# Ordering the crossed products of a half-chunk visit: a drain of TensorE in place of one-column ScalarE copies

## The chip, the cores and the metric

The kernel runs on one core of a Trainium2 chip. The metric is the device time of one execution in microseconds (us): the median of several executions, lower is better. The engines have the names that the profile gives them: PE is TensorE (matrix products), PEld its weight loads, ACT ScalarE, DVE VectorE, POOL GpSimd, SP the engine that issues most of the transfers. A q behind a name (PEldq, ACTq) means the engine's sequencer: instructions that never reach the engine's data path.

## The reference, cut to what matters

A retention layer over 4 batches, 8 heads, 768 positions and 64 channels a head is followed by two feed-forward layers (an ELU of width 2048, then a maximum over three products of width 768). Only the first concerns the change:

```python
for t in range(S):
    state = gamma * state + outer(k[:, :, t], v[:, :, t])
    y[:, :, t] = scale * (q[:, :, t] @ state)
```

## The kernel before

**Chunks and visits.** The recurrence is worked off in 24 chunks of 128 positions (6 chunks for each of 4 batches, taken batch by batch in turn, so that chunk c belongs to batch c % 4). Chunks 0 to 3 have no past and go through wider code at the start. Chunks 4 to 23 are worked in two halves of 64 positions with products of 64x64 tiles, four of which fit into the array of TensorE side by side. Such a half-chunk visit has these steps:

- `scores` (products at L207) and `update` (L235) of the chunk: keys times queries, and keys times values, both into the same two PSUM banks (tile `xs`).
- `mask` (DVE, L221), `decay` (POOL, L250), `advance` (DVE, L256 and L258) and `queries_of` (POOL, L194): the masked scores, the two states, and the decayed queries.
- `value_products` (L276 and, through `past(c, 0)`, L265): values times masked scores, then the straight part of queries times states, into two more PSUM banks, also named `xs`, one for each half s.
- `watch` (ACT, L289): one column of each of these two banks is copied into a spare column of `cols_sb`. Nothing reads the copies. They read the banks, so the crossed products that come next have to wait for them, and they themselves wait for the straight products.
- `finish_products` (L265 again, through `past(c, 1)`): the crossed part of queries times states is added into the same banks. The half s of the output now takes its rows from the other group of 64 rows of the array: `s = g ^ cross`. So a tile of another row group adds to the same PSUM columns as in the straight part.
- `finish_copies` and `finish_low` (L309, L316, L333) or `finish_row` (L1776): the result leaves PSUM.

One execution has 20 such visits. Each records 16 crossed products (16 instructions on PE at L265 and as many weight loads).

**The order of the work.** Chunks 4 to 7 stand in an order written out by hand (the string `FIRST`: V is `value_products`, gd is `watch`, F is `finish_products`, S and U are `scores` and `update`). Chunks 8 to 23 are put in order by a planner that has a cost and a due time for each step. It runs when the program is built; on the chip each engine has one fixed queue. In the plan a visit is

```python
def visit(c):
    value_steps(c)
    ...
        open_steps(c + 1)
    finish_steps(c)
```

with these steps for the copies and the crossed products:

```python
add("A", 0.42, lambda: watch(c), xs, [("seen", c)])
...
add("P", 0.45, lambda: finish_products(c), [("seen", c), mid, qd], xs + [("free", 0), ("home", c % CB)])
```

So between the straight and the crossed products of chunk c the queue of PE mostly has `scores` and `update` of chunk c + 1, which is small tiles again. In some visits the step just ahead of the crossed products is instead a product of a feed-forward layer, of the full 128x128 array with 512 columns (L481, L491, L504, L555). These full products fill the rest of PE's queue. L447 is ScalarE's half of the conversion of a weight, which full products at L491 wait for.

Of the kernel before, what the change touches and what calls it, by code (L numbers as in the profile page):

```python
# [78 lines left out]
def kernel(ctx: ExitStack, tc: tile.TileContext, qkv0, qkv, wa, wb, dmask, qdec, cols, out):  # L79


    nc = tc.nc
# [19 lines left out]
    guard = cols_sb[:, H + 2 * NPAIR:]  # L102
# [45 lines left out]
    def rows(i):  # L148
        return slice(i * HC, (i + 1) * HC)

    def heads():
        return [(2 * i + g, g, r, 2 * i + r) for i in range(2) for r in range(2) for g in range(2)]
# [107 lines left out]
    def past(c, cross):  # L260
        qd = st_t[c]
        for p, g, r, n in heads():
            s = g ^ cross
            src = middle if s else home[c % CB]
            nc.tensor.matmul(  # L265
                xo_t[c][s][rows(r), p, :], src[rows(g), n, :], qd[rows(g), n, s * HC:(s + 1) * HC],
                start=False, stop=p // 2 == 1, skip_group_check=True,
            )
# [13 lines left out]
    def values(c):  # L282
        value_products(c, twin()[0])
        watch(c)

    def watch(c):
        xs = xo_t[c]
        for s in range(2):
            nc.scalar.copy(guard[:, s:s + 1], xs[s][:, 0, 0:1])  # L289

    def finish(c):
        finish_high(c)
# [2 lines left out]
    def finish_high(c):  # L295
        finish_products(c)
        finish_copies(c)

    def finish_products(c):
        past(c, 1)  # L300
        if c // CB < NCH - 1:
            home[c % CB], free_state[0] = free_state[0], home[c % CB]
        del raw_t[c], st_t[c]
# [1256 lines left out]
    def low_copies():  # L1560
# [7 lines left out]
        "Uw": wide_update, "hm": wide_home, "S": early_scores, "K": keys_of, "U": lambda c: update(c, twins.pop(c)),  # L1568
        "M": mask, "mid": decay, "C": advance, "Q": queries_of, "V": lambda c: value_products(c, twin()[0]),
        "gd": watch, "F": finish_products, "xh": finish_copies, "xl": finish_low, "qk": lambda c: load(c, "qk"),  # L1570
        "k": lambda c: load(c, "k"), "v": lambda c: load(c, "v"), "kv": lambda c: load(c, "kv"),
        "bi": cv_bits, "sh": cv_shift, "sg": cv_sign, "tl": cv_tail, "hi": cv_high, "lo": cv_low,
# [171 lines left out]
    def value_steps(c):  # L1744
        su, a, mid, qd = opened[c]
        banks = [bank() for _ in range(2)]
        xs = [x for x, _ in banks]
        add(
            "P", 0.82, lambda: value_products(c, twin()[0]), [kv_of(c), a, mid, qd, ("home", c % CB)], xs,
            [x for _, x in banks],  # L1750
        )
        add("A", 0.42, lambda: watch(c), xs, [("seen", c)])
        opened[c] = xs, mid, qd

    def finish_steps(c):
        xs, mid, qd = opened[c]
        add("P", 0.45, lambda: finish_products(c), [("seen", c), mid, qd], xs + [("free", 0), ("home", c % CB)])
        late_c = c >= DEFER
        if c // CB == 3:
            for s in range(2):  # L1760
                add("A", 0.8, lambda s=s: finish_row(c, s), xs[s:s + 1], [("row", c, s)], [("X", 0)])
            if c % CB == CB - 1:
                for x in ("a21", "a22"):
                    plan.add("Q", 0.0, None, [("row", k, s) for k in range(c - CB + 1, c + 1) for s in range(2)], [("source", "a", x)])
        elif late_c:
            x, x0, _ = e_ring()
            add("A", 0.9, lambda: finish_high(c), xs, [x], [x0])
            add("S", 0.42, lambda: store_late(c), [x], [("xd", c)], move=(32, 0.032))
        else:
            add("A", 0.66, lambda: finish_high(c), xs, [("xh", c)], [("X", c // CB - 2)])  # L1770
            add("D", 0.76, lambda: finish_low(c), xs + [("xh", c)], [("xl", c)], [("X", c // CB - 2)])
# [333 lines left out]
```

## Time and profile before

| what | us |
| --- | --- |
| median of 3 executions (lowest, highest) | 946.17 (945.87, 948.68) |
| the profiled execution, its own time | 947.08 |
| span of its trace, first to last instruction | 945.3 |

The visits of chunks 4 to 7 lie between 30 and 57 us of the span, those of chunks 8 to 23 between 133 and 400 us; after that there are no half-chunk visits. In the rows below, times are in us from the start of the span. Engines work side by side, so that a busy engine matters for the time where the others wait for it in the end. A row of the timeline that merges several instructions gives the start of the first and the length to the end of the last.

### The profile page before, as it was taken

To read this page: it belongs to the slowest core of one execution; us is meant where nothing else is said; L and a number is where in the kernel's file an instruction comes from. 1 tells how busy PE (TensorE), PEld (TensorE's weight loads), DVE (VectorE), ACT (ScalarE), POOL (GpSimd) and SP (SyncE) were. 2 spreads that over 40 slices of the span, in tenths; PEclk is the share of its full clock that TensorE was granted. 3 is DMA by queue.
4 is the path that set the end of the run, shared out by engine and by line. 5 is a ranking of instruction groups with operands and counts; after the bars stand their busy time and mean duration, and the time that the engine had idled before them with its cause. 6 is when DMAs were issued, how large, how long until landed. Compare 5 with 4: busy or idle time off the path is not lost.

```text
span 945.3 us, 16772 instructions
## 1 busy us (share of the span) xinstructions
PE 932.2 (99%) x6553; PEld 764.1 (81%) x6553; DVE 653.5 (69%) x1009; ACT 379.8 (40%) x694; POOL 246.3 (26%) x346
## 2 busy tenths in 40 slices
PE   7999999999999999999999999999999999999998
PEld 5778888778788888888888888888888888888886
DVE  6897777667687576688668885898725777246651
ACT  3566554545564454556446663222311113101110
POOL 2510022554445245312333341345000100001000
PEclk9999999999999999999999999999999999999999
DMA  9924366789779498679777797989636564345602
GB/s 312 337 94 166 118 210 205 257 241 290 204 210 282 160 269 256 175 235 304 219 200 221 204 280 252 282 227 247 236 114 242 185 205 134 112 156 183 206 1 89
DMA packets 108351, 196.67 MB, mean 208 GB/s; under 512 B 8560, under 2 KB 53616, under 8 KB 104048
## 3 DMA queue, kind: packets, MB, share of 16 engines
q1 hardware_dynamic: 77296, 112.22, 36.3%
q0 software_dynamic: 29680, 80.76, 30.3%
q10 hardware_dynamic: 1296, 2.62, 0.8%
q8 instruction: 52, 0.85, 0.4%
q14 instruction: 27, 0.22, 0.1%
HBM read 141.30 MB, written 54.26 MB: 207 GB/s over the span
## 4 chain that ended last, share of the span: by engine, by line
PE 92%; DMA 3%; DVE 1%; issue 1%; POOL 1%; SPq 1%; ACT 1%; POOLq 0%; DVEq 0%
PE acc L555 22%; PE hp L1412 18%; PE hp L1204 12%; PE acc L1472 10%; PE acc L491 6%; PE hp L481 5%; PE hp L504 4%; PE acc L1313 3%; PE hp L1313 3%; PE hp L1268 2%; PE xs L276 1%; PE xs L265 1%; DMA ops_a<-t 1%; PE acc L1204 1%; PE xs L207 1%
## 5 line engine op out<-in xcount | busy, mean ns | idle before, releaser
L1412 PE MATMUL hp<-seat,w 128*128 128x512 f32 x798 | 182.4, 389 | 0.1
L1412 PEld LDWEIGHTS hp<-seat,w 128*128 128x128 f32 x798 | 149.6, 188 | 31.7 <-DMA w<-ops_d 0.5
L555 PE MATMUL acc<-gh,w 128*128 128x512 f32 x600 | 150.5, 392 | 0.0
L555 PEld LDWEIGHTS acc<-gh,w 128*128 128x128 f32 x600 | 111.7, 188 | 23.8 <-ACT gh L537 0.3
L1021 POOL DMA_DIRECT2D w<-ops_d x95 | 50.8, 537 | 280.1 <-PE hp L1412 209.9
L1204 PE MATMUL hp<-seat,w 128*128 128x512 f32 x504 | 115.9, 389 | 0.0
L1204 PEld LDWEIGHTS hp<-seat,w 128*128 128x128 f32 x504 | 94.6, 188 | 19.6
L1472 PE MATMUL acc<-w,g 128*128 128x512 f32 x432 | 99.1, 389 | 0.0
L1472 PEld LDWEIGHTS acc<-w,g 128*128 128x128 f32 x432 | 81.1, 188 | 16.8
L555 PE MATMUL acc<-gl,w 128*128 128x512 f32 x300 | 81.2, 390 | 0.0
L1010 POOL DMA_DIRECT2D w<-ops_a x91 | 49.4, 544 | 87.4 <-PE hp L1204 64.9
L555 PEld LDWEIGHTS acc<-gl,w 128*128 128x128 f32 x300 | 56.2, 188 | 11.8
L1438 ACT COPY u<-hp 128x512 f32<-128x512 f32 x19 | 11.2, 587 | 103.1 <-PE hp L1412 103.1
L184 POOL TENSOR_TENSOR x<-x,cols_sb 128x512 f32<-128x512 f32 x24 | 28.6, 1194 | 91.4 <-DMA x<-in_qkv 91.3
L541 DVE TENSOR_TENSOR gl<-e,gh 128x512 fp32r<-128x512 f32 x59 | 44.5, 755 | 9.9 <-ACT gh L537 4.1
L537 ACT CAST gh<-e 128x512 fp32r<-128x512 f32 x59 | 36.5, 619 | 33.7 <-PE acc L555 13.7
L874 POOL TENSOR_TENSOR t<-t 128x256 f32<-128x256 f32 x36 | 32.6, 906 | 66.3 <-DVE m L918 48.6
L491 PE MATMUL acc<-gh,w 128*128 128x512 f32 x168 | 44.8, 396 | 0.4 <-ACT gh L537 0.4
L504 PE MATMUL hp<-xh,w 128*128 128x512 f32 x120 | 39.4, 391 | 0.0
L1313 PE MATMUL hp<-seat,w 128*128 128x512 f32 x168 | 38.9, 390 | 0.0
L1313 PE MATMUL acc<-seat,w 128*128 128x512 f32 x168 | 38.7, 389 | 0.0
L541 DVE TENSOR_TENSOR gl<-hold,gh 128x512 fp32r<-128x512 f32 x32 | 24.5, 766 | 20.5 <-PE acc L555 20.3
(182 smaller groups left out, 1600.6 us busy)
## 6 DMA issues: line engine op xcount, KB each, us to landing
w<-ops_d POOLq DMA_DIRECT2D x33, 1024.0 KB, 5.2
w<-ops_a POOLq DMA_DIRECT2D x91, 256.0 KB, 4.3
x<-in_qkv SPq DMA_DIRECT2D x44, 512.0 KB, 5.8
ops_d<-m SPq DMA_DIRECT2D x66, 256.0 KB, 4.2
raw<-in_wa SPq DMA_DIRECT2D x32, 512.0 KB, 6.1
w<-ops_d POOLq DMA_DIRECT2D x63, 256.0 KB, 4.6
raw<-in_wb SPq DMA_DIRECT2D x24, 512.0 KB, 5.2
ops_a<-w SPq DMA_DIRECT2D x24, 256.0 KB, 3.7
```

Of the source, the lines that this page charges most:

```text
L481: nc.tensor.matmul(hp_t[b, f], w_t[0, f // 2][:, f % 2, pw, kk * P:(kk + 1) * P], x_t[b][px][:, kk, :], start=i == 0 and kk == 0, stop=i = ...
L491: nc.tensor.matmul(acc_t[b, f0][m], w_t[1, f // 2][:, f % 2, pw, m * P:(m + 1) * P], g_t[b, f][pg], start=f == f0 and i == 0, stop=f == f1 ...
L504: nc.tensor.matmul(hp, w[:, pw, kk * P:(kk + 1) * P], x[px][:, kk, :], start=k == 0, stop=k == len(order) - 1,)
L537: nc.scalar.copy(gh, e_t[b, f])
L541: nc.vector.tensor_tensor(out=gl, in0=e_t.pop((b, f)), in1=f32(gh), op=ALU.subtract)
L555: nc.tensor.matmul(acc_t[b, f0][m], w[:, p[0], m * P:(m + 1) * P], g[p[1]], start=f == f0 and p == first, stop=f == f1 - 1 and p == final, ...
L1010: nc.gpsimd.dma_start(out=live_slot(j).rearrange("p h t -> p (h t)"), in_=ops_a[:, j % AHEAD].rearrange("p h t -> p (h t)"))
L1021: nc.gpsimd.dma_start(out=group_tile(n)[:, a:z].rearrange("p s h t -> p (s h t)"), in_=ops_d[:, 4 * k + a:4 * k + z].rearrange("p s h t -> ...
L1204: nc.tensor.matmul(ps[name], w[:, pw, kk * P:(kk + 1) * P], x[px][:, kk, :], start=first and k == 0, stop=last and k == 5, skip_group_chec ...
L1313: nc.tensor.matmul(ps[name], w[:, pw, kk * P:(kk + 1) * P], x[px][:, kk, :], start=first and i == 0, stop=last and i == 5, skip_group_chec ...
L1412: nc.tensor.matmul(o, w[:, pw, kk * P:(kk + 1) * P], x[px][:, kk, :], start=first and k == 0, stop=last and k == 5, skip_group_check=True,)
L1472: nc.tensor.matmul(acc, g2[f][:, px, m * P:(m + 1) * P], w[:, pw, :], start=f == 0 and i == 0, stop=f == KF2 - 1 and i == 2, skip_group_ch ...
```

## The change

The step `watch` keeps its place and its cost in the plan but issues nothing. `finish_products` begins with a drain on TensorE's queue.

```diff
     def watch(c):
         xs = xo_t[c]
-        for s in range(2):
-            nc.scalar.copy(guard[:, s:s + 1], xs[s][:, 0, 0:1])
+        pass
...
     def finish_products(c):
+        nc.tensor.drain()
         past(c, 1)
         if c // CB < NCH - 1:
             home[c % CB], free_state[0] = free_state[0], home[c % CB]
```

## Rows read from the trace of the kernel before

**Rows 1.** The page: busy time and share of each engine, PE clock, chain

```profile
PE 932.2 (99%) x6553; PEld 764.1 (81%) x6553; DVE 653.5 (69%) x1009; ACT 379.8 (40%) x694; POOL 246.3 (26%) x346
...
PEclk9999999999999999999999999999999999999999
...
PE 92%; DMA 3%; DVE 1%; issue 1%; POOL 1%; SPq 1%; ACT 1%; POOLq 0%; DVEq 0%
```

**Rows 2.** Busy time by stretch: stretch, length, then PE busy (instructions) first

```profile
60.00:237.00 177.00, 176.23 (x1708) 143.84 (x1707) 132.38 (x216) 97.01 (x194) 50.70 (x52) 1.00 0.67 208
237.00:260.00 23.00, 21.79 (x222) 17.59 (x224) 15.20 (x26) 12.82 (x26) 10.43 (x16) 1.00 0.71 199
260.00:400.00 140.00, 139.96 (x1436) 115.60 (x1437) 98.86 (x151) 69.39 (x138) 57.37 (x78) 1.00 0.77 225
```

**Rows 3.** The copies' line: engine, operation, count, shortest/median/longest ns

```profile
L289 ACT COPY cols_sb<-xs x40: 141/160/167, 31.7 to 397.3; 128x1 f32<-128x1 f32 x40
```

**Rows 4.** PE's waits, 60 us to the end: total us, times, longest

```profile
PE xs L276 <- DVE e L1166: 0.9, 1, 0.9
PE xs L265 <- ACT cols_sb L289: 0.9, 2, 0.6
PE xs L207 <- DVE e L529: 0.2, 1, 0.2
```

**Rows 5.** Timeline around the crossed products of chunk 18: start, length, instruction

```profile
298.60 0.22 ACT L289 COPY cols_sb<-xs 128x1 f32<-128x1 f32 x2 [0.24 <-PE xs L265]
...
299.22 0.14 PEld L265 LDWEIGHTS xs<-qd,dmask_sb 64*64 64x64 f32 x1
...
299.29 0.22 PE L235 MATMUL xs<-x 64*64 64x64 f32 x1
299.34 0.40 PE L265 MATMUL xs<-qd,dmask_sb 64*64 64x64 f32 x14
299.67 0.50 PE L555 MATMUL acc<-gh,w 128*128 128x512 f32 x1
```

**Rows 6.** Timeline, the drains and the last products at the program's end

```profile
940.62 0.84 PE L1472 MATMUL acc<-w,g 128*128 128x512 f32 x3
941.50 0.37 ACT L1485 COPY o<-acc 128x256 f32<-128x256 f32 x1 [3.45 <-PE acc L1472]
```

**Rows 7.** PE's drains in the prologue and at the end: ns, first and last start

```profile
L2096 PEldq DRAIN x1: 8/8/8, 0.3 to 0.3; - x1
...
L2101 PEldq DRAIN x2: 13/2140/4267, 937.2 to 944.8; - x2
```

**Rows 8.** The chain of waits around the crossed products of chunk 16

```profile
258.81 0.28 PE xs L265 x13
259.10 0.21 ACT cols_sb L289 x2
259.31 0.04 issue
259.35 0.46 PE xs L265 x16
```

**Rows 9.** The same pattern as rows 5, its first and last place: chunks 8 and 22

```profile
135.55 0.22 PE L265 MATMUL xs<-qd,dmask_sb 64*64 64x64 f32 x1
135.56 0.22 PE L235 MATMUL xs<-x 64*64 64x64 f32 x1
...
390.13 0.22 PE L265 MATMUL xs<-qd,dmask_sb 64*64 64x64 f32 x1
390.13 0.22 PE L235 MATMUL xs<-x 64*64 64x64 f32 x2
```

**Rows 10.** Timeline before the crossed products of chunk 23

```profile
398.14 1.08 PE L555 MATMUL acc<-gh,w 128*128 128x512 f32 x4
399.15 0.29 PE L265 MATMUL xs<-qd,dmask_sb 64*64 64x64 f32 x4
...
399.15 0.15 PEld L265 LDWEIGHTS xs<-qd,dmask_sb 64*64 64x64 f32 x4 [0.36 <-issue]
```

**Rows 11.** The chain around the crossed products of chunk 5

```profile
42.80 0.46 PE xs L265 x16
43.26 0.02 issue
43.28 0.38 ACT xh L316
43.66 0.02 issue
43.69 0.76 DVE xl L333 x2
```

**Rows 12.** Timeline around the crossed products of chunk 6

```profile
47.86 0.64 PE L207 MATMUL xs<-x 64*64 64x64 f32 x30
...
49.04 0.50 PE L491 MATMUL acc<-gl,w 128*128 128x512 f32 x1 [0.24 <-DVE gl L541]
```

**Rows 13.** The chain around the crossed products of chunk 13

```profile
189.26 0.11 ACT cols_sb L289 x2
189.37 0.53 ACT w L447
189.90 0.04 issue
189.94 3.04 PE acc L491 x12
```

## Prediction

> **What bounds the kernel now.** I read the page first. PE is busy 932.2 us of a span of 945.3 us, its clock is at the top level in every slice, and the chain that ended last runs over PE for 92% of the span [rows 1]. The busy times by stretch then show how little room PE leaves where the planned visits lie: it is idle 0.8 us in the 177 us up to 237 us, 1.2 us in the next 23 us, and 0.04 us in the 140 us from 260 to 400 us [rows 2]. So in these stretches a step that holds PE for 0.1 us costs the kernel 0.1 us, and a step taken from another engine gains only what PE had waited for it. That is the key to the whole case: ScalarE is at 40% [rows 1], and what it is relieved of has no value of its own.
>
> Next I read what the copies cost. There are 40 of about 160 ns, two in each of the 20 visits [rows 3]. Together that is 40 x 0.16 = 6.4 us of ScalarE. PE waited for them twice after 60 us, 0.9 us in all; its only other two waits there came from VectorE, 0.9 and 0.2 us [rows 4]. In the other visits the copies were done long before PE came to the crossed products. In chunk 18 they run from 298.60 to 298.82, and the crossed products' first weights are loaded at 299.22 [rows 5]: scores and update of the next chunk lie between and cover the copies.
>
> **The change, part by part.**
>
> **The price of a drain.** The trace has drains on PE, at the program's two ends. With nothing in flight one took 8 ns, another 13 ns [rows 7]. The one at 937.2 us took 4.27 us and so ended at about 941.5 us [rows 7]; the last product of the program ends at 940.62 + 0.84 = 941.46 [rows 6]. So the drain was taken up by the sequencer four microseconds ahead of the array, and it ended when the last result was in, not when the last product had been issued. How long after, the rows give to 0.05 us only; ScalarE, which waits for the same product, starts 0.04 us after its end [rows 6], and I take 0.04 us for the drain too. Behind it the sequencer has to start again. The nearest row is PE's start behind the copies in chunk 16: the copies end at 259.31, the crossed products start 0.04 us later [rows 8]. I take 0.04 us for that as well. The drain's tail and restart then are 0.08 us, on top of the wait until the products in flight have ended. From below the bound is 0: results in, next load at once. From above I take the longest idle time that the rows show in front of a first weight load that waits for no other engine, 0.36 us [rows 10], with 0.04 us ahead of it, 0.40 us.
>
> **Eleven visits where small tiles run ahead** (chunks 8 to 11, 14 and 17 to 22; rows 5 show one, rows 9 the first and the last). The crossed products now overlap the update's: their weights are loaded at 299.22, while the last update product runs from 299.29 to 299.51, and all of the crossed ones end at 299.74 [rows 5]. Behind a drain they start at 299.51 + 0.08 = 299.59. Started from a standstill the 16 take 0.46 us [rows 8], so they end at 300.05 in place of 299.74: 0.31 us. Nothing covers this, since the full product at 299.67 [rows 5] stands behind them in PE's queue. Eleven times 0.31 is **+3.4 us** (0.23 x 11 = 2.5 with the lower bound, 0.63 x 11 = 6.9 with the upper).
>
> **Six visits where a full product runs ahead** (chunks 4, 5, 7, 12, 15 and 23). In chunk 23 the last full product ends at 399.22 and the crossed products' weights are loaded from 399.15 on [rows 10]. The array is changed from one tile size to the other here, and the overlap is only 0.07 us. With the drain the load comes at 399.22 + 0.08 = 399.30: 0.15 us, six times **+0.9 us** (0.4 to 2.8). The Trainium skill, "TensorEngine Tiling (Array Packing)", section Key Properties, says that a change of the tiling mode drains TensorE by itself; by it these six drains would add nothing. The overlap of 0.07 us in the modelled ends neither proves nor excludes that; it is a rival below. For the early ones delay is not hidden either: behind chunk 5 the chain itself leads from the crossed products over ScalarE's and VectorE's copies back to PE [rows 11].
>
> **Chunk 6: nothing.** Its predecessor, a run of score products, ends at 48.50; with 0.08 and 0.46 us behind it the crossed ones end at 49.04, which is when PE went on anyway, after a wait of 0.24 us for VectorE [rows 12]. With the upper bound it would cost 0.3 us.
>
> **The two visits where PE waited for the copies.** In chunk 16 the straight products end at 259.09 and the crossed ones started at 259.35 [rows 8]; behind a drain they start at 259.17, so I count **-0.2 us**. In chunk 13 PE waits for ScalarE in any case: the full products behind the crossed ones need a converted weight, which ends the chain at 189.90, and the copies stand ahead of it on ScalarE with 0.11 us of the chain [rows 13]. That is all there is to gain: **-0.1 us**. The wait of 0.5 us ahead of these crossed products was covered by that one, and so is the drain.
>
> **What is queued behind a drain.** PE's own products and weight loads, and the sequencer's waits; nobody waits for the drain itself. The copies out of the banks, the next decay on POOL and the load of the chunk after next wait for the crossed products and move with them. They keep their distance to PE's later steps, which move by the same amount. The 6.4 us taken from ScalarE hide beside PE and I cost them at nothing apart from the 0.1 us above; if PE were not the bound they would matter.
>
> **The sum** is 3.4 + 0.9 - 0.2 - 0.1 = +4.0 us. Against the profiled execution's own 947.08 us, of which 945.3 us are the span, this gives 951.1 us. That execution is 0.9 us above the median of the three runs, 946.17 us; against the median it gives **950.2 us**, 0.42% more. A difference under 0.3%, 2.8 us, can't be told from none.
>
> **The rivals.**
>
> *The tile size's own drain.* If a change of tile size empties the array already, six drains are free, and the sum is 3.1 us: 949.3 us. For it speaks that the load ahead of the crossed products stands idle for 0.36 us there [rows 10], against it the overlap of 0.07 us.
>
> *The drain does not hold the array.* If in mid-stream it ends when the products ahead of it are issued, it costs the sequencer 8 to 13 ns [rows 7], which its head start covers, and only gains are left: 0.1 us of chunk 13 and, in chunk 16, the whole time from 258.81 + 0.28 = 259.09 to 259.35 and the overlap of about 0.25 us that rows 5 show for unhindered crossed products. That is -0.6 us, 945.6 us, not slower than before. It is decided at the eleven small-tile places: by whether the crossed products still start 0.01 us ahead of the last update product [rows 9]. Against it speaks the drain of 4.27 us [rows 7].
>
> *The restart is dear.* The drain takes the sequencer's head start away; if each first load behind it comes as late as in rows 10, the upper bound holds: 6.9 + 2.8 + 0.3 us, little gained in chunk 16 either, together about +9.9 us, 956.1 us. Against it: PE's restart of 0.04 us behind the copies [rows 8], though there the products were already queued behind the wait.
>
> *ScalarE's relief reaches PE.* If other waits of PE shrank because ScalarE is free sooner and the drains were nearly free, the 2.0 us of rows 4 would be all that can go: 944.2 us. Three of them end on other engines' work or are counted above.
>
> **How the numbers follow.** The forecast has 0.57, the tile size's own drain 0.15, the drain that does not hold 0.10, the dear restart 0.13, ScalarE's relief 0.05. By 2.8 us slower are the dear restart (0.13), nine tenths of the forecast (0.51) and half of the tile-size case (0.08): 0.72. Faster by more than that would need more than all of PE's waits after 60 us; runs that scatter and the relief leave 0.04. The rest, 0.24, is within 0.3%. The range reaches from 946.5 us, which leaves out most of the drain that does not hold and the relief, to 953.5 us, which takes in a restart of up to 0.25 us a drain and leaves out the dear one at its full price. The forecast alone would lie between 948.7 us (lower bounds: 2.5 + 0.4 - 0.3 - 0.1 = +2.5) and 951.5 us.
>
> **What would show it.** Right: 20 drains on PE's sequencer that end just behind the last product ahead of them; at the eleven small-tile places the first crossed load 0.05 to 0.1 us after the last update product's end, and 0.3 us more from the straight products to the next full one; no overlap of crossed and other small products anywhere; no copies at L289, and no PE wait for them; nothing new between 400 us and the end. Wrong: an unbroken stream across the drain; a gap of 0.3 us or more between a drain's end and the first load; a new wait of PE for another engine behind the crossed products; or gaps at full-product places as long as at the small ones.

## The result and the profile after

The changed kernel takes 952.76 us, the median of 4 runs (952.44 to 953.82), beside 946.44 us of the kernel before on the same chip (4 runs, 945.87 to 948.68). The medians differ by 6.3 us. The ratio as recorded is 1.0061, with a 95% interval of 1.0045 to 1.0077: worked out from it, the change is 5.8 us (4.3 to 7.3) slower. The profiled execution of the changed kernel took 953.82 us, with a span of 952.1 us; that is 6.8 us longer than the span of the kernel before, 945.3 us.

The page of the changed kernel, engines and chain (it answers to [rows 1]):

```profile
PE 936.3 (98%) x6553; PEld 766.5 (81%) x6553; DVE 654.4 (69%) x1009; ACT 375.8 (39%) x654; POOL 247.3 (26%) x346
...
PE 94%; DMA 2%; SPq 1%; DVE 1%; issue 1%; ACT 1%; POOL 0%; POOLq 0%; DVEq 0%; ACTq 0%
```

ScalarE has 40 instructions and 4.0 us less and PE has the same 6553 products, but 4.1 us more busy time, and drains are not counted as busy; where that comes from is seen below. First the drain's line in the changed kernel (duration shortest/median/longest in ns, first and last start), for the whole program and then for chunk 18 alone:

```profile
L299 PEldq DRAIN  x20: 475/525/3752, 31.6 to 403.8; - x20
...
L299 PEldq DRAIN  x1: 517/517/517, 304.2 to 304.2; - x1
```

The sequencer waits 0.5 us in a typical drain. That is not its price: most of it is time in which the array still works off what was issued. The price is read from the array's own stream. Timeline of the changed kernel around the crossed products of chunk 18 (PE), with their first weight load (PEld); it answers to [rows 5]:

```profile
304.21 0.46 PE L235 MATMUL xs<-x 64*64 64x64 f32 x18
304.81 0.46 PE L265 MATMUL xs<-qd,dmask_sb 64*64 64x64 f32 x16
305.20 0.50 PE L555 MATMUL acc<-gh,w 128*128 128x512 f32 x1
...
304.80 0.15 PEld L265 LDWEIGHTS xs<-qd,dmask_sb 64*64 64x64 f32 x4 [0.28 <-issue]
```

The update's last product ends at 304.21 + 0.46 = 304.67. The crossed products' weights used to be loaded 0.29 us ahead of that end [rows 5]; now they are loaded 0.13 us behind it. From that end to the full product behind was 0.16 us before (299.51 to 299.67); it is 305.20 - 304.67 = 0.53 us now. This place cost 0.37 us.

The same view of the changed kernel at chunk 23, where a full product runs ahead (answers to [rows 10]):

```profile
405.53 0.62 PE L555 MATMUL acc<-gh,w 128*128 128x512 f32 x2
406.24 0.29 PE L265 MATMUL xs<-qd,dmask_sb 64*64 64x64 f32 x4
...
406.23 0.15 PEld L265 LDWEIGHTS xs<-qd,dmask_sb 64*64 64x64 f32 x3 [0.51 <-issue]
```

The full product ends at 406.15 and the load comes 0.08 us behind it; before, it came 0.07 us ahead: 0.15 us.

PE's waits in the changed kernel from 60 us on (total us, times, longest; answers to [rows 4]):

```profile
PE xs L276 <- DVE e L1166: 1.9, 1, 1.9
PE acc L491 <- ACT w L447: 0.5, 1, 0.5
PE xs L265 <- issue: 0.5, 3, 0.2
PE xs L207 <- DVE e L529: 0.2, 1, 0.2
```

The wait for the copies is gone. Its 0.6 us of chunk 13 came back in the line for ScalarE's converted weight (L447), which stood right behind it. The wait for VectorE ahead of chunk 16 grew from 0.9 to 1.9 us. The chain of the changed kernel around it:

```profile
248.12 6.90 DMA x2d<-o
...
255.89 4.44 DMA ops_a<-t
...
260.42 0.55 DVE t L781
...
261.03 0.69 DVE e L1166
...
261.76 0.62 PE xs L276 x24
```

PE waits there for VectorE, VectorE for a buffer whose store has to land, and the store took 4.44 us; the same store in the trace of before took 3.89 us. Behind that wait the clock fell. Busy time by stretch in the changed kernel (stretch, length, PE, PEld, VectorE, ScalarE, POOL, granted clock, DMA share, GB/s; answers to [rows 2]):

```profile
60.00:237.00 177.00, 175.32 (x1698) 142.47 (x1698) 131.37 (x215) 95.38 (x178) 50.26 (x51) 1.00 0.65 201
237.00:262.90 25.90, 23.91 (x210) 19.33 (x213) 15.77 (x27) 13.12 (x24) 10.29 (x15) 1.00 0.79 229
262.90:266.40 3.50, 3.50 (x82) 3.15 (x83) 2.04 (x6) 1.67 (x5) 3.27 (x5) 0.51 0.69 201
266.40:410.00 143.60, 142.66 (x1388) 117.21 (x1387) 100.32 (x152) 69.07 (x124) 56.10 (x75) 1.00 0.76 221
```

From 262.9 to 266.4 us the granted clock is 0.51, the lower level of 1.2 GHz, after PE had stood for 1.9 us. That time counts as busy, and so does the overlap that a drain takes away: in chunk 18, 0.14 of the 0.37 us are idle (304.67 to 304.81), and in the rest small products run one after another that ran side by side before. Eleven times 0.23, six times 0.06 (0.15 less the 0.09 us from 406.15 to 406.24) and 1.3 us of the lower clock, worked out below, make the 4.1 us by which PE's busy time grew, to within 0.1 us.

**The account of the profiled executions**, each place measured as above (after minus before, from the last product ahead of the crossed ones to the first behind them):

| part | forecast us | measured us |
|---|---|---|
| 11 small-tile places | +3.4 (0.31 each) | +4.1 (0.37 to 0.39 each) |
| 6 full-product places | +0.9 (0.15 each) | +0.9 (0.15 five times, 0.18 once) |
| chunk 6 | 0 | 0.0 |
| chunk 13 | -0.1 | 0.0 |
| chunk 16 | -0.2 | -0.1, at the lower clock |
| sum of the 20 places | +4.0 | +4.9 |
| longer wait ahead of chunk 16 (1.9 - 0.9) | none | +1.0 |
| lower clock behind it | none | +1.3 |
| all else | none | -0.4 |

The lower clock's 1.3 us come from the delay against the trace of before. It was 3.68 us at the end of chunk 16's straight products (by the timelines 262.73 against 259.05) and 5.18 us behind chunk 17's crossed ones (287.58 against 282.40). Of these 1.50 us, +0.37 belong to chunk 17's drain and -0.14 to chunk 16, and 1.3 us are left. The places explain 4.9 of the 6.8 us. The experiments ask whether that account of the drain holds and whose the other 2 us are: brought by the change, or chance that the kernel before has as well.

### The profile page after: what moved, and what is told of

It is laid out like the page before. It is cut to its first block, busy times and chain, and to the rows that moved or that the text cites. A ratio compares the mean times of both kernels' runs of the same rounds, so it can differ in the third digit from the quotient of the medians.

```text
span 952.1 us, 16749 instructions
## 1 busy us (share of the span) xinstructions
PE 936.3 (98%) x6553; PEld 766.5 (81%) x6553; DVE 654.4 (69%) x1009; ACT 375.8 (39%) x654; POOL 247.3 (26%) x346
## 4 chain that ended last, share of the span: by engine, by line
PE 94%; DMA 2%; SPq 1%; DVE 1%; issue 1%; ACT 1%; POOL 0%; POOLq 0%; DVEq 0%; ACTq 0%
PE acc L555 21%; PE hp L1412 19%; PE hp L1204 12%; PE acc L1472 10%; PE acc L491 6%; PE hp L481 5%; PE hp L504 4%; PE hp L1313 4%; PE acc L1313 4%; PE hp L1268 2%; PE xs L265 1%; PE xs L276 1%; PE xs L207 1%; PE xs L235 1%; PE acc L1204 1%; DMA x<-in_qkv 1%
```

## The experiments

Each ran beside runs of the kernel before on its own chip; its ratio is against those, and a difference in us that stands beside a ratio is worked out from it. The expectations number their theories anew, so that theory 1 of one is not theory 1 of another.

### Is the rest chance? The kernel before, once more

No edit.

> The kernel before, unchanged. It shows what of the 2.2 us that the changed kernel lost beside its drains is chance: the wait of PE ahead of chunk 16's value products (0.91 us before, 1.90 us after) and a stretch at half the clock behind it (none before, 3.4 us after). Theory 1 (both follow from the drains, which push PE against the transfers): the wait is 0.8 to 1.2 us and the clock full throughout, ratio 1.000. Theory 2 (both are chance, and come in any execution): the wait differs by 0.5 us or more between executions, and half-clock stretches are found in some of them too, in a mean clock of 0.996 to 0.999.

946.87 us, 0.9997 (0.9984 to 1.001). The waits of this execution from 60 to 950 us, and its stretch behind chunk 16's wait:

```profile
PE xs L277 <- DVE e L1167: 1.3, 1, 1.3
...
PE hp L1413 <- DMA w<-ops_d: 0.5, 1, 0.5
```

```profile
260.40:263.90 3.50, 3.50 (x64) 3.02 (x65) 2.19 (x4) 1.88 (x5) 3.34 (x5) 0.51 0.75 225
```

The unchanged kernel shows a wait of 1.3 us at the same place and the clock at 0.51 behind it. Neither needs a drain. A single pair of traces had made both look like the change's work. Whether drains make such waits longer on the average is not shown.

### What is the copies' removal worth? The drain with the copies kept

```diff
 before, in finish_products:
+        nc.tensor.drain()
         past(c, 1)
```

> The drains are added, the copies stay: the change without its removal. Theory 1 (the drains are the cost, the copies had hidden beside PE): +6 to +7 us, within 0.5 us of the changed kernel or slower than it by 0.3 us (chunks 13 and 16 then wait for copies and drain). Theory 2 (an idle ScalarE runs ahead and its stores collide with others, so that the removal costs part of it): +4 to +5 us, the rest being what the removal costs.

954.17 us, 1.0073 (1.0047 to 1.0098), no better and no worse than the change itself as far as 6 runs tell. The places cost 0.37 and 0.15 us as in the change; at chunks 13 and 16 nothing is gained. The 40 instructions taken from ScalarE have no value that the runs can tell.

This pair of kernels also shows what a drain's end depends on. At chunk 13 the same straight products (64x64) stand ahead of the drain in both; here ScalarE's copies wait for the last of them, in the changed kernel nobody does. The drain of chunk 13 in the changed kernel and here:

```profile
L299 PEldq DRAIN  x1: 475/475/475, 190.5 to 190.5; - x1
```

```profile
L300 PEldq DRAIN  x1: 528/528/528, 192.6 to 192.6; - x1
```

It takes 53 ns longer where an engine waits for the product ahead of it, and at chunk 16 the difference is 53 ns too (485 and 538).

### What is a drain when nothing is in flight? A second drain behind the first

```diff
 after, in finish_products:
         nc.tensor.drain()
+        nc.tensor.drain()
```

> The changed kernel with a second drain right behind each first one. If the price of a drain is to wait for the products in flight, the second finds an empty array and costs what a drain takes there, 0.01 to 0.06 us: +0.2 to +1.2 us on the changed kernel. If the price is a fixed one of the sequencer (0.15 us or more for any drain, empty or not), it is +2.5 us or more.

953.67 us, 1.0071 (1.0046 to 1.0096). The line of the second drain, and PE's timeline at chunk 18:

```profile
L300 PEldq DRAIN  x20: 13/13/13, 33.6 to 404.2; - x20
```

```profile
301.59 0.64 PE L235 MATMUL xs<-x 64*64 64x64 f32 x30
302.44 0.46 PE L265 MATMUL xs<-qd,dmask_sb 64*64 64x64 f32 x16 [0.22 <-issue]
302.84 2.11 PE L556 MATMUL acc<-gh,w 128*128 128x512 f32 x8
```

The second drain lasts 13 ns, as the empty one of [rows 7] did, but the crossed products start 302.44 - 302.23 = 0.21 us behind the update instead of 0.14, and the place costs 0.08 us more. Summed over the 20 places it is 6.4 us in place of 4.9, a little more than the 0.2 to 1.2 us that were expected. So a drain costs more than its own duration: only 0.01 us of the 0.08 is in its record. The whole runs do not show the 1.5 us (1.0071 beside 1.0061 for the change); they scatter by more.

### The gains alone: no copies and a drain at chunks 13 and 16 only

```diff
 before, in watch:
+        if c in (13, 16):
+            return
 in finish_products:
+        if c in (13, 16):
+            nc.tensor.drain()
```

> The change at chunks 13 and 16 alone, where PE had waited for the copies; elsewhere the copies stay and there is no drain. Theory 1: only the gain is left, -0.1 us in chunk 13 and -0.2 us in chunk 16, 0.3 us under the kernel before, too little to be told from none. If a drain is dear wherever it stands: +0.3 us or more.

947.90 us, 1.0007 (0.9997 to 1.0017). The trace has the two gains where the prediction put them and in its sizes, 0.11 us at chunk 13 and 0.22 us at chunk 16, and 0.00 us at the others. A third of a microsecond is below what 12 runs can tell; the profiled execution (949.27 us) had a longer wait ahead of chunk 16 too (1.1 us), and the clock fell behind it. The one version that keeps the gains without the costs is no faster.

### The changed kernel once more

No edit.

> The changed kernel once more, on the same chip as the three below. By the sites of its first trace the drains cost 4.9 us net (4.1 at the eleven small-tile places, 0.9 at the six full-product places, nothing in chunk 6, -0.1 in chunks 13 and 16 together). Theory 1 (the drains are the only lasting cost, the rest of the first +6.3 us was chance: a longer wait ahead of chunk 16 and a stretch at half the clock): +4.5 to +5.5 us over the kernel before. Theory 2 (the later arrival of PE also lengthens waits for transfers in most executions): +6 to +7 us.

954.28 us, 1.0078 (1.0057 to 1.0099), 7.4 us by the ratio and 7.7 by the medians. The places come to 4.9 us again. Both theories had expected 7 us at most. This time chunk 16's wait was 1.0 us and the clock stayed at the top, as chance allows; but PE stood in a new place. Timeline of PE from 46 us in this execution:

```profile
47.39 0.45 PE L276 MATMUL xs<-a,x 64*64 64x64 f32 x12
49.19 0.51 PE L276 MATMUL xs<-a,x 64*64 64x64 f32 x18 [1.35 <-issue]
```

In the middle of chunk 6's value products PE stands 1.35 us and waits for nothing that the profile shows. The first changed run had these products in one piece.

### The two kinds of places alone

```diff
 drain_small, before, in finish_products:
+        if c in (8, 9, 10, 11, 14, 17, 18, 19, 20, 21, 22):
+            nc.tensor.drain()
 drain_full, before, in finish_products:
+        if c in (4, 5, 7, 12, 15, 23):
+            nc.tensor.drain()
```

(The copies stay in both.)

> Copies everywhere, drains at the eleven places with small tiles ahead alone. Theory 1: 11 x 0.37 = +4.1 us, with each of these places 0.37 us longer in the trace. Theory 2: +5 us or more, with longer waits ahead of chunk 16 and near 670 us. If the drains work on ScalarE's or VectorE's order in any other way, places without a drain change by over 0.05 us.

> Copies everywhere, drains at the six places with a full product ahead alone. Theory 1: 6 x 0.15 = +0.9 us, with each place 0.15 us longer. The rival that a change of the tile size drains the array by itself: 0 to +0.3 us, with the first load behind a drain no later than 0.02 us after the last full product.

Small-tile places alone: 951.02 us, 1.0042 (1.003 to 1.0054), which is +4.0 us (2.8 to 5.1); by the trace the places sum to 4.1. Full-product places alone: 947.39 us, 1.0007 (0.9999 to 1.0016), about +0.7 us, which is not clear of none in whole runs; by the trace 1.0. One place without a drain did change by more than the expectation's 0.05 us: at chunk 16 PE waited 0.44 us for the copies with drains at the small-tile places and 0.55 us with drains at the others, 0.30 us before. Why was not followed up. PE's timeline at chunk 18 with drains at the small-tile places:

```profile
301.09 0.46 PE L235 MATMUL xs<-x 64*64 64x64 f32 x18
301.69 0.46 PE L265 MATMUL xs<-qd,dmask_sb 64*64 64x64 f32 x16
302.08 0.50 PE L557 MATMUL acc<-gh,w 128*128 128x512 f32 x1
```

The update ends at 301.55, the full product comes at 302.08: 0.53 us again. Together the two kinds make 4.7 us by the ratios, the price of the drains as whole runs show it.

The profiled execution of the full-product variant, 950.86 us, was its slowest run. PE's timeline from 46 us, and its clock behind that:

```profile
47.50 0.45 PE L276 MATMUL xs<-a,x 64*64 64x64 f32 x11
50.81 0.73 PE L276 MATMUL xs<-a,x 64*64 64x64 f32 x19 [2.86 <-issue]
```

```profile
50.90:54.30 3.40, 3.40 (x88) 3.09 (x88) 1.24 (x4) 1.11 (x5) 0.83 (x2) 0.51 0.02 5
```

The stand of chunk 6 again, 2.9 us, and the clock at 0.51 behind it: some 4.3 us of this execution's delay arise there, not at the drains.

### Do added products ahead of chunk 16 keep the clock up?

```diff
 after, ahead of chunk 16's value products:
+        for _ in range(3 if c == 16 else 0):
+            for p, g, r, n in heads():
+                for s in range(2):
+                    nc.tensor.matmul(
+                        banks[s][rows(r), p, :], v[rows(s), p, r, :], v[rows(s), p, r, :],
...
```

The added products stand in front of the real ones and are no part of the reference's work.

> The changed kernel with three rounds of value products of chunk 16 (1.4 us of small tiles, keys' place taken by the values themselves) put ahead of the real ones into the same banks, which then overwrite them: work in the place of PE's wait there. Theory 1 (the idle wait lets the clock fall to half behind it): no half-clock stretch at chunk 16, 1.0 to 1.5 us less than the changed kernel in executions where it had one, some 0.5 us less in the median. If the clock falls for another reason, or the fill is longer than the wait: 0 to +0.5 us.

954.79 us, 1.0074 (1.006 to 1.0088): no gain, a miss. The profiled execution (961.22 us) had PE stand 2.8 us near 48 us and a wait of 2.2 us at chunk 16 all the same, and the clock fell behind both. Where the second wait lies shows why:

```profile
PE xs L277 <- DVE e L1173: 2.2, 1, 2.2
```

L277 is the line of the added products. They write the same banks as the real ones and waited for the same VectorE instruction, so the edit put work behind the wait and not in its place. Whether work in its place keeps the clock up was not tested.

### Which drains go with the stand at 48 us?

Chunks 4 to 7 lie in the part of the program whose order is written out by hand. Three edits split it: a drain at chunks 4 and 5, one at chunk 5 alone (all copies kept in both), and the change everywhere but there (`EARLY` is 8).

```diff
 head_only, before, in finish_products:
+        if c in (4, 5):
+            nc.tensor.drain()
 five_only, before, in finish_products:
+        if c == 5:
+            nc.tensor.drain()
 no_head, before, in watch:
+        if c >= EARLY:
+            return
 in finish_products:
+        if c >= EARLY:
+            nc.tensor.drain()
```

> Copies everywhere, drains at chunks 4 and 5 alone. Theory 3 (a drain in the hand-ordered head holds PE's sequencer while the next 16 KB block of its instructions is due; in some executions that block then comes at 47 to 49 us in place of 42 us and PE stands still for 1.4 to 5 us ahead of chunk 6's value products): +0.3 us directly, and 1.5 to 5 us more in a third to two thirds of the executions, so a median of +0.3 to +3 us and a spread of 4 us or more. Rival (such stalls come with any kernel, or with drains anywhere): a median of +0.3 us and a spread no wider than that of the kernel before, 2.5 us.

> Copies everywhere, a drain at chunk 5 alone; the sequencer is held by it from 41.5 to 43.0 us, when the block of 42 us is fetched. Theory 3: +0.15 us directly and the same late stalls as with both drains of the head. If the drain at chunk 4 (31.6 to 33.7 us) or the two together are needed: +0.15 us, no fetch later than 43 us and no stall.

> The change from chunk 8 on; chunks 4 to 7 keep their copies and have no drain. Theory 3: only the direct price is left, 4.9 us less 0.15, 0.15 and 0.18 for chunks 4, 5 and 7, that is +4.4 us (+3.9 to +5), no stall near 48 us, and a spread of some 2.5 us as in the kernel before. Rival (the rest of the loss comes from the places behind chunk 8 too): +6 us or more.

Drains at 4 and 5: 947.04 us, 0.9997 (0.9988 to 1.0006), with no loss and a spread of 2.1 us, against theory 3. At 5 alone: 950.18 us, 1.0023 (1.001 to 1.0037), with its 11 runs in two groups, five from 946.98 to 948.39 and six from 950.18 to 952.06; the slowest of 21 runs of the kernel before beside them took 949.40. Both profiled executions show chunk 6's products in one piece. Without any drain in the head: 951.82 us, 1.005 (1.0038 to 1.0063), +4.7 us, five runs within 1.7 us. Its waits from 20 to 950 us:

```profile
PE xs L276 <- DVE e L1170: 1.1, 1, 1.1
...
PE xs L265 <- issue: 0.5, 3, 0.2
```

Nothing stands at L276 for "issue". The places sum to 4.4 us here, chunk 16 gives its 0.22 us, chunk 13 nothing.

Chunk 5 alone was run again, with no other edit:

> The kernel with a drain at chunk 5 alone, once more, for a second profile: the first one fell on an execution without a stall, though the times spread from 946.98 to 952.06 us. Theory 3: again a spread of 4 us or more, and if the profiled execution is one of over 950 us, its block of instructions comes at 46 us or later and PE stands still for 1.4 us or more ahead of chunk 6's value products. Rival: the slow executions lose their time elsewhere, at chunk 16 or near 670 us, with the block at 42 us as before.

947.52 us, 1.0016 (1.0002 to 1.0029), beside 947.16 us of the kernel before; eight of 12 runs up to 947.96, four from 949.77 to 951.83 (the kernel before: up to 949.22 in 17), and a profile of one of the eight. More than 2 us come and go from run to run with this single drain. No profile fell on an execution that had them, so where they arise is not shown. It is not shown either why the drains at 4 and 5 together, which contain this one, had no such run in 11.

## Why the prediction was right, and where it was off

Forecast 950.2 us (946.5 to 953.5) and slower at 0.72; measured 952.76 us. Direction and mechanism were right; 4.0 us were forecast against the kernel before, and 6.3 came. By the profile the drains' places account for 4.9 us. The rest comes from waits that the prediction did not have, and that the time still fell inside the range is in part luck: the second series of the same kernel, 954.28 us, lies above it.

**PE as the bound: right.** The copies' removal is worth nothing outside chunks 13 and 16 (the copies kept: 1.0073, taken away: 1.0061 and 1.0078), and what a drain adds to PE's stream at a planned visit stays in the time. ScalarE was relieved of 4.0 us, not of 6.4: the two copies of a visit overlap, and a pair takes 0.22 us [rows 5], not twice 0.16. As ScalarE is not the bound, the error had no effect.

**The drain waits for the results: right.** All 20 end behind the last product ahead of them, and no crossed product overlaps one ahead of it. (Behind it there is no drain: at chunks 5, 12 and 16 the next scores still start before the crossed products end.) The rival in which the drain does not hold the array is gone.

**Tail and restart, 0.08 us: too small at the small-tile places.** This is the step that was mis-sized. There the drain ends 0.08 to 0.10 us after the last small product's modelled end, where 0.04 was taken, and the first load comes 0.053 us after the drain's end, where 0.04 was taken: 0.135 to 0.156 us together, above the 0.05 to 0.1 us that the prediction named as its sign. So a place costs 0.37 to 0.39 in place of 0.31 us and eleven cost 4.1 in place of 3.4. At five of the six full-product places the drain ends 0.02 us after the product, the restart is 0.053 us, the sum 0.07, and the place costs the 0.15 us forecast.

The size of the tile is not what makes most of this difference. Behind the 64x64 products of chunks 13 and 16, which nobody waits for in the changed kernel, the tail is 0.03 us; with the copies waiting for them it is 0.08. In the eleven places VectorE waits for the update's end. The one full product of the six that another engine waits for, ahead of chunk 7, has 0.05 us, the place that costs 0.18. The row of 0.04 us that served as a price was ScalarE's start behind a full product [rows 6]. One price had been taken for all places, from a row that shows one kind.

**The tile size's own drain: fallen as a price, open as a mechanism.** With full products ahead the load moved from 0.07 us ahead of the last product's modelled end to 0.07 behind it, at 0.15 us a place, so these six drains are not free. That does not show that the array is not emptied by the change of tile size: the second drain of a pair finds the array empty and still costs 0.08 us, and the restart of 0.053 us comes on top: an estimate of 0.13 us for a drain of an empty array. Modelled ends can't tell the remaining 0.02 us from none.

**The dear restart: fallen.** It is 0.053 us, not 0.36. The idle time of 0.36 us in front of a load [rows 10] only says that the load had nothing to do while the full products ahead ran.

**The two gains: right in size, not always there.** Alone they come to 0.11 and 0.22 us, as forecast. In the whole change chunk 13's did not come: PE's wait for the weight (L447) took its place, 0.5 us, and the second time the place was 0.09 us dearer than before. Why ScalarE's conversion was no earlier there though the copies ahead of it were gone was not followed up.

**The sum.** By the ratios it is 4.0 + 0.7 = 4.7 us for the two kinds, and 4.7 us for the change without the head: the price of the drains by their places, 4.4 to 5.1 us. The whole change measured 5.8 us (4.3 to 7.3) and 7.4 us (5.4 to 9.4) the second time. So 1 to 3 us lie beyond the places; the first measurement alone would not tell them from none. They have two sources in the traces. The wait ahead of chunk 16 and the lower clock behind it are seen in the kernel before as well and differ from execution to execution: in the five profiles with all the drains the wait was 1.9, 1.6, 1.0 and 2.2 us and once absent, in the two of the kernel before 0.9 and 1.3. That much is chance; whether the drains lengthen the wait on the average is open. The stand at chunk 6 is not seen in any of the five profiles without a drain in the head, and in four of the nine with one. That points to the drains, but four stands dealt out at random among 14 profiles would miss these five in one case of eight, and the condition is open (last section). The prediction's list of what waits behind a drain named products, loads and the sequencer's waits; if the reading of the last section holds, it left out the instructions that the sequencer itself waits for.

## What to carry to other kernels

On the engine whose queue is the bound, a drain costs the rest of what is in flight, its tail and a restart, and nothing can be put in front of it; a wait for another engine's result that stands behind other work costs nothing while that work lasts. So ask of each place whether the present wait is exposed (here 2 of 20 were, 0.9 us in all, of which drains gave back 0.3) before replacing it, and take the price of a new wait from a row with the same kind of work ahead of it: the same tile size, and a last product that another engine waits for or not. A microsecond that one pair of traces shows and the places do not explain is looked for in a second execution of the kernel before, first.

## What the runs showed of the hardware

**A drain's tail depends on whether another engine waits for the last product ahead of it:** by modelled ends 0.08 to 0.10 us behind 64x64 products with a waiting engine and 0.03 us behind those without, 0.05 us (one place) and 0.02 us behind 128x512 ones. At chunks 13 and 16 the same products show both values, without and with the copies. And an empty drain recorded with 13 ns delays the stream by 0.08 us.

**The clock.** After PE had stood 1.9 us (the changed kernel), 1.3 us (the kernel before) and 2.9 us (drains at full products) the granted clock was 0.51 for about 3.5 us. The length of the stand alone does not decide it: behind 1.1 us at the same place the clock fell to 0.51 with the drains at chunks 13 and 16 only and stayed at 1.00 in the change without the head. And with the drain and the copies PE waited 1.6 us there, and the clock behind it was 1.00:

```profile
263.00:267.00 4.00, 3.21 (x128) 2.76 (x129) 3.06 (x6) 1.18 (x5) 2.61 (x4) 1.00 0.60 166
```

**Instruction blocks that come late.** The page lists an instruction queue, q8, with 52 packets and 0.85 MB in the program, 16 KB each; by their times I read them as PE's program. In the queue view of the changed kernel, from 40 to 46.5 us (packets, MB, share):

```profile
q8 instruction: 1, 0.02, 1.0%
```

All ten profiled executions without a stand at chunk 6 have this one packet in that stretch. The four with a stand have none there (the changed kernel the second time, the drains at full products, the drain with copies, the filled wait), and one behind it instead. From 46.5 to 50 us in the changed kernel the second time:

```profile
q8 instruction: 1, 0.02, 1.6%
```

That packet starts at 46.9 us there and PE goes on at 49.2; with drains at the full products it starts at 48.4, and PE goes on at 50.8. In all four PE goes on 2.2 to 2.4 us behind the packet's start, and in all four the stand falls at the same place of PE's queue, behind its 597th weight load. So in these four PE stood, by place and order of the times, for its own instructions, 1.4 to 2.9 us. All four have drains at chunks 4, 5 and 7, of which only 4 and 5 come ahead of the stand. In the changed kernel the second time the drain of chunk 5 held the sequencer from 41.5 to 43.0 us, just when the block comes in the other executions, at 42 us. That it puts the request off is argued, not shown, and it is not enough: the first time the same drain held the sequencer over the same stretch, and the block came at 42.1 us. Drains at 4 and 5 alone showed it in no profile and 11 close runs, one at chunk 5 alone scatters without a profile of it, and the changed kernel's first execution and the one with doubled drains had all 20 and no stand. What decides it from run to run stays open.
